# Six key chunks of a pair scored in one group of 64-row matmuls, and a new instruction order for attention and the experts

## The chip, the cores and the metric

The kernel runs on one core of a Trainium2 chip. The metric is the device time of one execution in microseconds (us). Engines are named as in the profile: PE (TensorE matmul), PEld (its weight load), DVE (VectorE), ACT (ScalarE), POOL (GpSimd), SP (SyncE, here a DMA queue).

## What is computed

Attention over four batches of eight heads (768 positions, head size 64), with a local band of |distance| < 16 and 24 block summaries per head; its result goes through a gate that is normalised eight times over rows and columns, and through eight experts that all see every token.

```python
k_sum = k.reshape(B, H, nb, 32, D).max(axis=3)
v_sum = v.reshape(B, H, nb, 32, D).mean(axis=3)
scores_l = scale * q @ k^T, kept where |i - j| < 16
scores_s = scale * q @ k_sum^T + log(32)
a = softmax(concat[scores_l, scores_s]);  x = a @ concat[v, v_sum]     # 3072 x 512
P = exp(x @ w_gate);  8 times: rows to 1, columns to N / E
out = sum over e of P[:, e] * (relu(x @ w1[e]) @ w2[e])                # 512 -> 1024 -> 512
```

## The kernel before

**Attention** works on 16 pairs of heads, four per batch. Pairs 0 to 3 (batch 0) go in halves of 384 positions (`pair_half`, L731), so that the first expert can start early; pairs 4 to 15 go whole (`pair_whole`, L761). The steps of a whole pair are: transposes of k and q (`tr`, `tr_out`; by a DMA transpose on SP from pair 12 on, `tr_dma`), `key_max`, `block_sums` and `block_out`, four small DMAs on SP (`near_values`), then for each half h: `scores` (three key chunks for each of the two heads), `score_exp` (ACT), `masks` (DVE); then `edges` (DVE), `summaries` and `summary_exp`, `values` (PE), `normalize` (DVE), and the transposition of x (`to_xT` and `x_out`, or `x_dma` on SP).

A score has a contraction of 64, so two heads share the array: head 0 uses rows 0 to 63 and head 1 rows 64 to 127 (`score_mm`, L388). All other matmuls, but the first transposes, use all 128 rows. `scores` writes head 0 into one bank of the two-bank PSUM buffer `s` and head 1 into the other (columns 0 to 479 of each):

```python
def scores(i, h):
    sg = at["sg", i, h] = banks2("sg")
    for s in range(HG):          # three chunks
        for j in range(2):       # two heads
            score_mm(i, sg[:, j, s * LIVE:(s + 1) * LIVE], j, HG * h + s, 0, LIVE)
```

PSUM has eight banks: `m` three, `a` three, `s` one buffer of two. Expert 0's products (`hidden0` into `m`, `project0` into `m`) are done as plain matmuls between the steps of attention, batch by batch, as its rows of x come in. Its relu and its copies out may go to ACT or DVE.

**The gate** needs all of x. Its eight normalisations (`bridge`, L1495) are a chain of small DVE, POOL and PE steps beside expert 0's last matmuls and expert 1's first ones. `bridge` starts with three 128x512 matmuls on zeros (L1498).

**Experts 1 to 7** use Winograd's seven products for both matrix products (`duo`, `pair`), in places with a second level (`second`, L1050; `twin`, L1378). Each product's PSUM bank is copied or combined by ACT and DVE between matmuls that go into it: `p1`, `seed`, `p2` and so on, in `plan_duo`; `q1`, `c1` (L1203), `q5`, `v5`, `q6`, `v6` (L1216) and so on in `plan_pair`. Results go out as accumulating DMAs on POOL (`da`, `db`, L1287 and L1290), and in the last block by SP and ACT queues (`store`, L1239).

**The order** is no written sequence. Each step is a unit with an engine, a cost in us, its dependencies, a priority and PSUM buffers; `Plan.order` (L60) puts units out one by one, always the one that can start first by those costs and, among those that can start within 0.02 us of it, the one of lowest priority value. A unit on PE that changes the shape of the array (64-row, 64-column or whole) costs `RESHAPE` = 0.1 more. Where PE would stand idle for over 0.22 us before the first relu, the planner puts in a 128x512 matmul on zeros (`keep_busy`, L597). The result is a fixed order of instructions on each engine; each engine takes its own in order and waits on semaphores. In attention the priorities are pair numbers; for the experts they are numbers in a table `PR`.

Of the kernel before, what the change touches and what calls it, by code (L numbers as in the profile page):

```python
# [36 lines left out]
class Plan:  # L37

    HOP = {"PE": 0.23}
    RESHAPE = 0.1  # L40

    def __init__(self, slots, idle=None):
        self.idle, self.shape = idle, None
        self.ring, self.free, self.waiting, self.now = {}, {}, [], []
        self.more(slots)
# [14 lines left out]
    def order(self):  # L60
# [3 lines left out]
        def hop(x, e):  # L64
            return 0.0 if x.on == e else self.HOP.get(x.on, 0.1)

# [20 lines left out]
        while waiting or left:  # L87
# [4 lines left out]
            for u in left:  # L92
                t0 = ready(u)
# [11 lines left out]
            for e, c in best.items():  # L105
                t_min = min(t for t, _, _ in c)
                t, u, cost = min((x for x in c if x[0] <= t_min + 0.02), key=lambda x: (
                    not (e == "PE" and self.shape and x[1].shape), x[1].prio))
                picks.append((t, t + cost, e, u, cost))
# [31 lines left out]
def kernel(  # L141
# [111 lines left out]
    if True:  # L253
# [175 lines left out]

        def score_exp(i, h):  # L430
# [262 lines left out]
        def pair_start(i, prio):  # L693
# [4 lines left out]
            for z in range(2 if i >= PB else 1):  # L698
# [9 lines left out]
                U["kT", i, z] = add({"ACT": 0.8} if z == 0 else {"ACT": 0.8, "DVE": 0.95},  # L708
# [4 lines left out]
            U["km", i] = add("DVE", 0.85, lambda: key_max(i), [U["kT", i, 0]] + war_q[2:], prio)  # L713
# [5 lines left out]
            U["Vs", i] = add("DVE", 0.24 if i < PB else 0.7, lambda: block_out(i), [U["vs", i]],  # L719
                             prio + 0.01, uses=[buf])  # L720

        def query_half(i, h, prio):
# [4 lines left out]
            U["kT", i, 1] = add({"ACT": 0.46, "DVE": 0.5}, 0, lambda: tr_qh_out(U["qT", i, h].on, i, h),  # L727
# [3 lines left out]
        def pair_half(i, h, prio):  # L731
            if h:
# [6 lines left out]
                               [U["kT", i, 0], U["kT", i, 1], hist("mk", n - 3), hold], prio, opens=[buf], shape="row")  # L739
            U["X", i, h] = add("ACT", 1.0, lambda: score_exp_h(i, h), [U["S", i, h]], prio, uses=[buf])  # L740
            U["mk", i, h] = add("DVE", 0.78, lambda: masks_h(i, h),
# [5 lines left out]
            U["sx", i, h] = add("ACT", 0.46, lambda: summary_exp(i, h), [U["ss", i, h]], prio, uses=[buf])  # L747
            buf = Buffer("a")
            U["A", i, h] = add("PE", 0.67, lambda: values_h(i, h),
                               [U["mk", i, h], U["sx", i, h], U["Vs", i]], prio, opens=[buf])  # L750
            U["no", i, h] = add("DVE", 0.68, lambda: normalize(i, h), [U["A", i, h], hist("xt", n - 2)],
                                prio, uses=[buf])
            buf = Buffer("a")
            U["xt", i, h] = add("PE", 0.172, lambda: to_xT(i, h), [U["no", i, h], U["gc"]], prio, opens=[buf])
            U["x", i, h] = add({"ACT": 0.46, "DVE": 0.5}, 0, lambda: x_out(U["x", i, h].on, i, h),
# [4 lines left out]

        def pair_whole(i, prio):  # L761
            U["near", i] = add("SP", 2.5, lambda: near_values(i), [U["v", i], U.get(("A", i - NE, 1))], prio,
                               lag=4.5)
            for h in range(2):
                buf = Buffer("s")
                U["S", i, h] = add("PE", 0.215, lambda h=h: scores(i, h),
                                   [U["kT", i, 0], U["kT", i, 1], U.get(("ed", i - 2))], prio, opens=[buf], shape="row")
                U["X", i, h] = add("ACT", 0.97, lambda h=h: score_exp(i, h), [U["S", i, h]], prio, uses=[buf])
                U["mk", i, h] = add("DVE", 0.56, lambda h=h: masks(i, h),
                                    [U["X", i, h], U.get(("A", i - 2, 1))], prio)  # L770
            U["ed", i] = add("DVE", 0.78, lambda: edges(i),
                             [U["X", i, 0], U["X", i, 1], U["mk", i, 1], U.get(("A", i - NE, 1))], prio)
            for h in range(2):
                buf = Buffer("a")
                U["ss", i, h] = add("PE", 0.17, lambda h=h: summaries(i, h, "a"),
                                    [U["km", i], U["kT", i, 1], U.get(("A", i - NE, 1))], prio, opens=[buf])
                U["sx", i, h] = add("ACT", 0.46, lambda h=h: summary_exp(i, h), [U["ss", i, h]], prio, uses=[buf])
            for h in range(2):
                buf = Buffer("a")
                U["A", i, h] = add("PE", 0.36, lambda h=h: values(i, h),  # L780
                                   [U["mk", i, h], U["ed", i], U["sx", i, h], U["Vs", i], U["near", i]],
                                   prio, opens=[buf])
                U["no", i, h] = add("DVE", 0.68, lambda h=h: normalize(i, h),
                                    [U["A", i, h], U.get(("xt", i - 2))], prio, uses=[buf])
# [3 lines left out]
            else:  # L788
                buf = Buffer("a")
                U["xt", i] = add("PE", 0.34, lambda: to_xT(i), [U["no", i, 0], U["no", i, 1]], prio, opens=[buf])  # L790
                U["x", i] = add({"ACT": 0.8, "DVE": 0.9}, 0, lambda: x_out(U["x", i].on, i), [U["xt", i]], prio,
# [4 lines left out]
        def expert0(t0, xs):  # L796
# [5 lines left out]
            for f in range(KF):  # L802
# [13 lines left out]
                U["rl", key, f] = add({"ACT": 0.5, "DVE": 0.56}, 0, ev, [m], -1.0, uses=[buf])  # L816
                evac.append(U["rl", key, f])
                zero.extend([m, evac[-1]])
            for c in range(HG):
# [9 lines left out]
                U["yo", key, c] = add({"ACT": 0.58, "DVE": 0.68}, 0, ev, [p1], -1.0, uses=[buf])  # L829
                zero.extend([p0, p1, U["yo", key, c]])  # L830

        def gate(b, xs, prio):
            buf = Buffer("a")
            U["lg", b] = add("PE", 0.61, lambda: logits(b), xs, prio, opens=[buf])
            U["lo", b] = add("ACT", 0.25, lambda: logits_out(b), [U["lg", b]], prio, uses=[buf])
# [72 lines left out]
        plan.idle = (0.22, lambda: keep_busy(1), U["rl", 0, 0])  # L908
        attention = {u for u in plan.waiting if u.fn is not None} - set(zero)
# [11 lines left out]
    if True:  # L921
# [444 lines left out]
        def twin(e, j, c, b0, b1):  # L1366
# [49 lines left out]
            def n4():  # L1416
# [4 lines left out]
        us = dict(m=0.1092, p=0.4316, q=0.4368, seed=0.55, c5=0.5, c2=0.49, r=0.49, c12=0.607, c22=0.607, s=0.6,  # L1421
                  n=0.2232, ns=0.6, nw=0.205, c1=0.34, v6=0.28, v5=0.35, y=0.395, half=0.275, join=0.335, w1=0.205, w2=0.6, wa=0.14, x=0.6,
                  xa=0.2, sc=0.63, part=0.36, da=1.0)
# [137 lines left out]
        for u in course:  # L1561
# [371 lines left out]
```

## Time and profile before

| what | value |
|---|---|
| median of three runs | 661.84 us (660.36 to 662.11) |
| the profiled execution | 661.13 us, of which the span from the first to the last instruction is 659.1 us |
| granted TensorE clock | 1.000 |
| PE busy | 650.6 us, 5575 matmuls |
| DVE busy | 546.6 us |
| ACT busy | 528.0 us |
| POOL busy | 260.2 us |
| DMA | 77.73 MB, 118 GB/s on average |

Attention with expert 0 between its steps takes the first 110 us; expert 0 alone with the gate goes on to 175 us; experts 2 to 6 repeat a pattern of 71.4 us; the last expert ends at 655 us, and DMAs to 659.1 us. A matmul's bar in the trace is longer than the time until the next one starts (matmuls are pipelined), so waits shorter than about 0.16 us do not show as idle time; they show in the distance between the starts of matmuls.

### The profile page before, as it was taken

How to read it: one execution, taken by the hardware profiler on the slowest of the kernel's cores; microseconds unless marked ns; L12 is line 12 of the kernel's file. 1: busy time of each engine (PE TensorE's matmuls, PEld its weight loads, DVE VectorE, ACT ScalarE, POOL GpSimd, SP SyncE). 2: the span in 40 equal slices, each digit the busy share in tenths (PEclk: the TensorE clock that was granted, in tenths of full speed). 3: DMA queues.
4: the chain of work that ended last, by engine and by line, in shares of the span. 5: the costliest groups of instructions: out<-in, count | busy, mean ns of one | idle time of the engine just before them, and what ended most of it. 6: DMA issues, size and time to landing. Idle time of an engine off the chain costs nothing.

```text
span 659.1 us, 15106 instructions
## 1 busy us (share of the span) xinstructions
PE 650.6 (99%) x5575; PEld 446.3 (68%) x5575; DVE 546.6 (83%) x1356; ACT 528.0 (80%) x1183; POOL 260.2 (39%) x320
## 2 busy tenths in 40 slices
PE   8999999999999999999999999999999999999997
PEld 4766656555677766676776776767767677676676
DVE  8889998678799979896898779877889689876876
ACT  6776766565996578889898898898989989888872
POOL 8599504223101022444345244433344335633421
PEclk9999999999999999999999999999999999999999
DMA  9999957700727357986989698977998699978758
GB/s 162 185 148 149 148 85 77 93 2 1 143 68 141 123 99 106 111 109 92 173 103 118 93 141 124 117 101 106 158 108 112 93 175 128 137 110 191 113 85 190
DMA packets 147368, 77.73 MB, mean 118 GB/s; under 512 B 112736, under 2 KB 125280, under 8 KB 147296
## 3 DMA queue, kind: packets, MB, share of 16 engines
q0 software_dynamic: 124864, 62.64, 80.9%
q1 hardware_dynamic: 21472, 13.68, 8.4%
q8 instruction: 43, 0.70, 0.5%
q10 hardware_dynamic: 960, 0.48, 0.3%
q14 instruction: 29, 0.24, 0.1%
HBM read 55.59 MB, written 45.09 MB: 153 GB/s over the span
## 4 chain that ended last, share of the span: by engine, by line
PE 86%; DVE 7%; DMA 3%; issue 1%; POOL 1%; ACT 0%; DVEq 0%; POOLq 0%
PE pab L992 16%; PE pg L992 16%; PE py L998 16%; PE px L998 13%; PE px L1378 7%; PE yps L236 5%; PE hps L226 5%; PE pab L1050 4%; DVE xs L552 1%; DMA kT<-kst 1%; DMA w<-in_moe_w_dram 1%; DMA kst<-in_k_dram 1%; PE sg L388 1%; PE tkq L354 1%; DVE em L440 1%
## 5 line engine op out<-in xcount | busy, mean ns | idle before, releaser
L998 PEld LDWEIGHTS <-hf 128*128 128x128 f16 x1840 | 178.4, 98 | 53.2
L1290 POOL DMA_DIRECT2D out_dram<-out_acc x68 | 62.0, 917 | 173.8 <-ACT out_acc L1266 141.2
L936 DVE TENSOR_TENSOR hf<-hf 128x1024 f16<-128x1024 f16 x142 | 94.6, 692 | 4.1 <-ACT hf L217 1.4
L998 PE MATMUL py<-w,hf 128*128 128x256 f16 x656 | 92.6, 273 | 0.0
L1287 POOL DMA_DIRECT2D out_dram<-out_acc x68 | 64.9, 955 | 56.3 <-ACT out_acc L1266 27.2
L942 DVE CUSTOM_DVE_ANT_0 hf<-pg,c 128x512 f16<-128x512 f32 x84 | 57.5, 684 | 28.5 <-PE pg L992 15.6
L1266 ACT ACTIVATE out_acc<-py,P_sb 128x256 f32<-128x256 f32 x136 | 65.3, 490 | 6.9 <-PE py L998 6.8
L992 PEld LDWEIGHTS <-ws 128*128 128x128 f16 x504 | 47.5, 98 | 31.6 <-issue 0.3
L202 POOL DMA_DIRECT2D w<-in_moe_w_dram x56 | 44.6, 844 | 49.1 <-PE pg L992 46.8
L992 PEld LDWEIGHTS <-w 128*128 128x128 f16 x520 | 48.1, 98 | 21.7 <-issue 0.6
L1116 ACT COPY c<-pab 128x512 f32<-128x512 f32 x84 | 50.1, 596 | 15.9 <-PE pab L992 14.5
L942 DVE CUSTOM_DVE_ANT_0 hf<-pab,c 128x512 f16<-128x512 f32 x84 | 57.5, 685 | 6.2 <-ACT c L1123 3.4
L998 PE MATMUL px<-ws,hf 128*128 128x256 f16 x400 | 59.8, 273 | 0.0
L217 ACT ACTIVATE hf<-pg 128x512 f16<-128x512 f32 x84 | 50.6, 602 | 11.3 <-PE pg L992 10.5
L998 PE MATMUL px<-w,hf 128*128 128x256 f16 x400 | 59.3, 273 | 0.0
L992 PE MATMUL pab<-xT,w 128*128 128x512 f16 x184 | 54.4, 379 | 0.0
L1108 ACT COPY pg<-pab 128x512 f32<-128x512 f32 x84 | 49.7, 592 | 3.4 <-PE pab L1050 3.0
L1123 ACT COPY c<-pg 128x512 f32<-128x512 f32 x84 | 49.7, 591 | 3.3 <-PE pg L992 1.5
L217 ACT ACTIVATE hf<-pab 128x512 f16<-128x512 f32 x84 | 49.8, 610 | 3.0 <-PE py L998 2.0
L992 PE MATMUL pg<-xTs,w 128*128 128x512 f16 x168 | 50.0, 379 | 0.1
L992 PE MATMUL pg<-xTs,ws 128*128 128x512 f16 x168 | 50.0, 379 | 0.0
L992 PE MATMUL pab<-xT,ws 128*128 128x512 f16 x168 | 50.0, 379 | 0.0
(190 smaller groups left out, 1511.2 us busy)
## 6 DMA issues: line engine op xcount, KB each, us to landing
out_dram<-out_acc POOLq DMA_DIRECT2D x136, 256.0 KB, 5.1
w<-in_moe_w_dram POOLq DMA_DIRECT2D x8, 1024.0 KB, 11.2
w<-in_moe_w_dram POOLq DMA_DIRECT2D x56, 128.0 KB, 5.0
out_dram<-out_acc SPq DMA_DIRECT2D x28, 256.0 KB, 2.3
vx<-in_v_dram POOLq DMA_DIRECT2D x16, 192.0 KB, 5.8
qst<-in_q_dram POOLq DMA_DIRECT2D x31, 96.0 KB, 5.3
kst<-in_k_dram POOLq DMA_DIRECT2D x24, 96.0 KB, 5.4
out_acc<-out_dram SPq DMA_DIRECT2D x8, 256.0 KB, 4.0
```

What stands on the lines that cost most here:

```text
L217: nc.scalar.activation(out=out, in_=in_, func=AF.Relu, bias=0.0, scale=1.0)
L936: nc.vector.tensor_tensor(out=out, in0=in0, in1=in1, op=ALU.subtract)
L942: nc.vector._custom_dve(TENSOR_ADD_SAT, out=out, in0=in0, in1=in1, s0=FLT_MAX, s1=0.0)
L992: nc.tensor.matmul(bank[:], lhsT=w[:, dk, :], rhs=x[:, dk, :], start=start and dk == 0, stop=dk == KH - 1, skip_group_check=True)
L998: nc.tensor.matmul(bank, lhsT=a(f)[:, 128 * c:128 * (c + 1)], rhs=w[:, f, :], start=start and f == 0, stop=f == FH - 1, skip_group_check=True)
L1108: nc.scalar.copy(out=B["g" + K][:], in_=B["a" + K][:])
L1116: nc.scalar.copy(out=B["c5" + K][:], in_=B["b" + K][:])
L1123: nc.scalar.copy(out=B["c2" + K][:], in_=B["g" + K][:])
L1266: nc.scalar.activation(out=out_acc[:, (c, HT + c)[t == tb], k * DH:(k + 1) * DH], in_=at(src), func=AF.Copy, scale=scale[:, t, e:e + 1])
L1287: nc.gpsimd.dma_start(out=rows(ta), in_=out_acc[:, c, :], accum_op=ALU.add)
L1290: nc.gpsimd.dma_start(out=rows(tb), in_=out_acc[:, HT + c, :], accum_op=ALU.add)
L1378: nc.tensor.matmul(half(b, k)[:, g, :], lhsT=still2(e, j, g, w, c)[:, i, :], rhs=moving2a(e, g, v)[:, i, :], start=start and g == 0 and i ...
```

## The change

The scores of a whole pair are one unit of twelve matmuls instead of two of six. Chunks 0 to 2 still go to the buffer `s`; chunks 3 to 5 go to one `m` bank (head 0) and one `a` bank (head 1). The exponential of the first half stays one instruction over both heads (128x960); that of the second half becomes two of 128x480. `scores_h` of pairs 0 to 3 is as before.

```diff
+def scores_all(i):
+    sg = at["sg", i, 0] = banks2("sg")
+    one = at["sg", i, 1] = [bank(t, "sg") for t in ("m", "a")]
+    for h in range(2):
+        for s in range(HG):
+            for j in range(2):
+                dst = one[j][:, s * LIVE:(s + 1) * LIVE] if h else sg[:, j, s * LIVE:(s + 1) * LIVE]
+                score_mm(i, dst, j, HG * h + s, 0, LIVE)
+
+def score_exp_j(i, j):
+    nc.scalar.activation(out=at["er", i][:, j, HG:G, :].rearrange("p g l -> p (g l)"),
+                         in_=at["sg", i, 1][j][:, 0:HG * LIVE], func=AF.Exp, bias=0.0, scale=SCALE)
...
 def pair_whole(i, prio):
+    bufs = [Buffer("s"), Buffer("m"), Buffer("a")]
+    U["S", i, 0] = U["S", i, 1] = add("PE", 0.43, lambda: scores_all(i), [...], prio, opens=bufs, shape="row")
+    U["X", i, 0] = add("ACT", 0.97, lambda: score_exp(i, 0), [U["S", i, 0]], prio, uses=bufs[:1])
+    ex = [add("ACT", 0.48, lambda j=j: score_exp_j(i, j), [...], prio, uses=bufs[1 + j:2 + j]) for j in range(2)]
+    U["X", i, 1] = add("LAND", 0, None, ex, lag=-0.1)
     for h in range(2):
-        buf = Buffer("s")
-        U["S", i, h] = add("PE", 0.215, lambda h=h: scores(i, h), [...], prio, opens=[buf], shape="row")
-        U["X", i, h] = add("ACT", 0.97, lambda h=h: score_exp(i, h), [U["S", i, h]], prio, uses=[buf])
         U["mk", i, h] = add("DVE", 0.56, lambda h=h: masks(i, h), [...])
```

The rest changes what the planner works with, and so the order alone: other costs, other waits between engines, a dependency of each step on the same step of the pair before (S, X, A, no, xt), a table `RANK` of some 400 numbers added to the priorities of attention's units, a new `PR` table (same names, other numbers), w1 loads reckoned as 4.3 us, and, in the Winograd sums, T3 or S3 no longer depending on the sum before it (`PREV`).

```diff
-    HOP = {"PE": 0.23}
+    HOP = {"PE": 0.23, "ACT": 0.15, "DVE": 0.14}
...
-U["rl", key, f] = add({"ACT": 0.5, "DVE": 0.56}, 0, ev, [m], -1.0, uses=[buf])
+U["rl", key, f] = add({"ACT": 0.39, "DVE": 0.475}, 0, ev, [m], -1.0, uses=[buf])
...
+RANK = {"k": -3.72, "q0": 5.3, "q0.0": 12.32, "v": 16.47,
...
+for key, u in U.items():
+    if isinstance(key, tuple) and u not in seen and u in plan.waiting:
+        kind = key[0] + "".join(str(x) for x in key[2:])
+        u.prio += RANK.get(kind, 0.0) + RANK.get(f"{kind}.{key[1]}", 0.0)
...
-us = dict(m=0.1092, p=0.4316, q=0.4368, seed=0.55, c5=0.5, c2=0.49, r=0.49, ..., c1=0.34, v6=0.28, v5=0.35,
+us = dict(m=0.1092, p=0.4316, q=0.4368, seed=0.53, c5=0.48, c2=0.48, r=0.485, ..., c1=0.27, v6=0.29, v5=0.335,
...
 def bridge():
-    for n in (0, 1, 0):
+    for n in (0, 1):
         nc.tensor.matmul(t[n][:], lhsT=zeros[:], rhs=zeros[:, None, :].to_broadcast([128, 4, 128]),
+    plan.HOP, plan.window = {"PE": 0.23}, 0.02
...
 PR = {
-    "m1": 2568.5, "m5": 1010.4, "m2": -2957.6,
+    "m1": -1176448.7, "m5": -881981.4, "m2": -883425.6,
...
+plan.SAME = {"DVE": 0.07}
+PREV = (None, 0, 0, 1)
```

In the two orders as built, compared engine by engine: PE has the same matmuls but for `bridge` (two on zeros instead of three) and `keep_busy` (27 on zeros instead of 24). Ten relus of expert 0 (of 17), three 128x384 copies and one 128x512 copy move from DVE to ACT. POOL's first 157 instructions (waits not counted), all of attention's loads among them, stand as before. On SP the k transposes of pairs 13 and 14, and q transposes with them, stand ahead of `near_values` of pairs 10 and 11.

More of the change, by code (lines that the diff above doesn't have):

```diff
@@ L37 @@
 class Plan:
[L39 removed]
+    HOP = {"PE": 0.23, "ACT": 0.15, "DVE": 0.14}
     RESHAPE = 0.1
+    SAME = {}
     def __init__(self, slots, idle=None):
[L43 removed]
+        self.idle, self.shape, self.window = idle, None, 0.02
         self.ring, self.free, self.waiting, self.now = {}, {}, [], []
@@ L707, in pair_start @@
                                     prio, opens=[buf], shape="col" if i < PB else None)
-                U["kT", i, z] = add({"ACT": 0.8} if z == 0 else {"ACT": 0.8, "DVE": 0.95},
+                U["kT", i, z] = add({"ACT": 0.7} if z == 0 else {"ACT": 0.7, "DVE": 0.475},
                                     0, lambda z=z: tr_out(U["kT", i, z].on, i, z), [U["tr", i, z]], prio,
@@ L712, in pair_start @@
                 query_half(i, 0, prio)
-            U["km", i] = add("DVE", 0.85, lambda: key_max(i), [U["kT", i, 0]] + war_q[2:], prio)
+            U["km", i] = add("DVE", 1.14, lambda: key_max(i), [U["kT", i, 0]] + war_q[2:], prio)
             if i == 0:
@@ L726, in query_half @@
                                 opens=[buf], shape="col")
-            U["kT", i, 1] = add({"ACT": 0.46, "DVE": 0.5}, 0, lambda: tr_qh_out(U["qT", i, h].on, i, h),
+            U["kT", i, 1] = add({"ACT": 0.4, "DVE": 0.475}, 0, lambda: tr_qh_out(U["qT", i, h].on, i, h),
                                 [U["tr", i, 1]], prio, uses=[buf])
@@ L738, in pair_half @@
             U["S", i, h] = add("PE", 0.225, lambda: scores_h(i, h),
-                               [U["kT", i, 0], U["kT", i, 1], hist("mk", n - 3), hold], prio, opens=[buf], shape="row")
-            U["X", i, h] = add("ACT", 1.0, lambda: score_exp_h(i, h), [U["S", i, h]], prio, uses=[buf])
-            U["mk", i, h] = add("DVE", 0.78, lambda: masks_h(i, h),
+                               [U["kT", i, 0], U["kT", i, 1], hist("mk", n - 3), hist("S", n - 1), hold], prio, opens=[buf], shape="row")
+            U["X", i, h] = add("ACT", 0.9, lambda: score_exp_h(i, h), [U["S", i, h], hist("X", n - 1)], prio, uses=[buf])
+            U["mk", i, h] = add("DVE", 0.71, lambda: masks_h(i, h),
                                 [U["X", i, h], U["band"], hist("A", n - NEH), clear], prio)
@@ L759, in hist, with before @@
             return U.get((what, n % PB, n // PB)) if n >= 0 else None
+        def before(what, i, h):
+            return U[what, i, 0] if h else U.get((what, i - 1, 1))
         def pair_whole(i, prio):
@@ L780, in pair_whole @@
                 U["A", i, h] = add("PE", 0.36, lambda h=h: values(i, h),
-                                   [U["mk", i, h], U["ed", i], U["sx", i, h], U["Vs", i], U["near", i]],
+                                   [U["mk", i, h], U["ed", i], U["sx", i, h], U["Vs", i], U["near", i], before("A", i, h)],
                                    prio, opens=[buf])
-                U["no", i, h] = add("DVE", 0.68, lambda h=h: normalize(i, h),
-                                    [U["A", i, h], U.get(("xt", i - 2))], prio, uses=[buf])
+                U["no", i, h] = add("DVE", 0.7, lambda h=h: normalize(i, h),
+                                    [U["A", i, h], U.get(("xt", i - 2)), before("no", i, h)], prio, uses=[buf])
             if 10 <= i < 15:
@@ L790, in pair_whole @@
                 U["xt", i] = add("PE", 0.34, lambda: to_xT(i), [U["no", i, 0], U["no", i, 1]], prio, opens=[buf])
-                U["x", i] = add({"ACT": 0.8, "DVE": 0.9}, 0, lambda: x_out(U["x", i].on, i), [U["xt", i]], prio,
+                U["x", i] = add({"ACT": 0.7, "DVE": 0.475}, 0, lambda: x_out(U["x", i].on, i), [U["xt", i]], prio,
                                 uses=[buf])
@@ L828, in ev @@
                     copy(U["yo", key, c].on, out_acc[:, t0 // 128 + c, :], at.pop(("yp", key, c))[:])
-                U["yo", key, c] = add({"ACT": 0.58, "DVE": 0.68}, 0, ev, [p1], -1.0, uses=[buf])
+                U["yo", key, c] = add({"ACT": 0.485, "DVE": 0.61}, 0, ev, [p1], -1.0, uses=[buf])
                 zero.extend([p0, p1, U["yo", key, c]])
@@ L1674, in h_sub_sums @@
                                       [src[0]["s2"], src[0]["s3"]], [])):
-                s.append(put("DVE", us["ns"], lambda n=n: h_sub(e, j, n), s[-1:] + more, prio + 0.01 * n))
+                s.append(put("DVE", us["ns"], lambda n=n: h_sub(e, j, n), ([s[PREV[n]]] if n else []) + more, prio + 0.01 * n))
         def w2_sub_sums(e, prio, old=()):
```

62 lines of the change are left out of this document (37 added, 25 removed), and 200 rows, old and new, of tables (PR, RANK).

## Prediction

> **What bounds the kernel now.** First the page's head, its busy shares and the chain that ended last.
>
> ```profile
> span 659.1 us, 15106 instructions
> ...
> PE 650.6 (99%) x5575; PEld 446.3 (68%) x5575; DVE 546.6 (83%) x1356; ACT 528.0 (80%) x1183; POOL 260.2 (39%) x320
> ...
> PE 86%; DVE 7%; DMA 3%; issue 1%; POOL 1%; ACT 0%; DVEq 0%; POOLq 0%
> ```
>
> PE is busy for 99% of the span and makes up 86% of the chain: PE's own time is the kernel's time. Work taken from DVE or ACT is worth nothing unless PE waits for it. Then busy times by stretch: start, attention with expert 0, gate, experts to 597 us, last expert, tail.
>
> ```profile
> 0.00:21.00 21.00, 18.00 (x243) 10.49 (x244) 16.80 (x100) 12.93 (x20) 17.36 (x28) 1.00 1.42 169
> 21.00:126.00 105.00, 104.00 (x1165) 65.68 (x1164) 92.07 (x279) 74.03 (x127) 60.33 (x76) 1.00 1.56 130
> 126.00:175.00 49.00, 49.00 (x282) 27.52 (x280) 35.60 (x83) 31.77 (x62) 13.37 (x19) 1.00 0.24 39
> 175.00:597.00 422.00, 421.83 (x3407) 299.77 (x3406) 357.16 (x807) 367.71 (x879) 150.33 (x178) 1.00 0.81 117
> 597.00:655.00 58.00, 57.73 (x486) 42.83 (x484) 43.96 (x88) 41.52 (x98) 18.78 (x22) 1.00 0.78 143
> 655.00:659.10 4.10, 0.00 (x0) 0.00 (x0) 1.00 (x3) 0.00 (x0) 0.00 (x0) 1.00 0.57 196
> ```
>
> The columns are the stretch, its length, then busy time (and count) of PE, PEld, DVE, ACT, POOL. PE has no idle time worth a name from 21 to 655 us. What can be won is of three kinds: PE time that does no work though PE looks busy, the start, and 4.1 us behind the last matmul. For the first I read PE's timeline round two score groups.
>
> ```profile
> 53.97 1.02 PE L236 MATMUL yps<-w,h 128*128 128x512 f16 x4
> 54.92 0.38 PE L388 MATMUL sg<-qT,kT 64*128 64x160 bf16 x6
> 55.24 1.90 PE L236 MATMUL yps<-w,h 128*128 128x512 f16 x8
> 56.98 0.35 PE L463 MATMUL av<-vx,em 128*128 128x65 bf16 x6
> ```
>
> The eight `yps` matmuls start 56.98 - 55.24 = 1.74 us before what follows, 0.217 each. The four ahead of the scores take 54.92 - 53.97 = 0.95, so 0.95 - 4 x 0.217 = 0.08 to 0.10 us (0.096 in the unrounded starts) pass when PE goes from whole array to 64 rows. The six scores take 0.32: two heads start 0.003 apart, so three pairs at 0.069 make 0.21, and 0.11 is left, again 0.096 for the way back and 0.01 for the first pair. A group thus pays 0.19 us for its two changes, whatever its length.
>
> The start, and a wait in the experts:
>
> ```profile
> 15.11 0.34 PE L475 MATMUL ss<-qT,ksT 128*128 128x384 bf16 x1
> 15.81 0.34 PE L559 MATMUL tx<-ident,xs 128*128 128x128 f16 x3 [0.36 <-DVE xs L552]
> ...
> 20.79 0.65 PE L226 MATMUL hps<-xT,w 128*128 128x384 f16 x3
> ```
>
> ```profile
> 305.95 1.04 PE L998 MATMUL py<-w,hf 128*128 128x256 f16 x8
> ...
> 306.52 0.43 DVE L939 TENSOR_TENSOR pab<-pab,m 128x256 f32<-128x256 f32 x1
> ...
> 307.00 0.27 PE L1050 MATMUL pab<-xT,wa 128*128 128x256 f16 x1
> ```
>
> Expert 0's first matmuls start at 20.79; until then PE mostly follows loads and DVE. In the experts eight matmuls at 0.109 end issue at 306.82, and PE goes on at 307.00, 0.05 after the DVE join ended: 0.18 us that a busy bar hides. Summed over all starts between 174 and 655 us, such waits come to 2.3 us, of them 0.9 behind 597 us.
>
> **The change part by part.** (1) *Grouped scores.* Twelve pairs lose one group each: 24 changes of shape. In the two orders PE changes shape 74 times before and 50 after. 24 x 0.096 = -2.30 us. It lies on the path, since PE is without idle time there. Below it could be 0 only if the second six paid as much inside the group; inner distances in the groups of eight of pairs 0 to 3 (0.066 to 0.069 a pair throughout) speak against that.
>
> (2) *One matmul on zeros less* in `bridge`: 512 columns, -0.22 us.
>
> (3) *Split exponential.* From 478 ns (64x384) and 970 ns (128x960) a line gives 560 ns for 128x480: 24 x 0.56 - 12 x 0.97 = +1.8 us of ACT. Ten relus (0.49), three copies (0.48) and one wide copy (0.59) come from DVE: +6.9. ACT in 21 to 126 us goes from 74.0 to 82.7 of 105, DVE from 92.1 to some 84 (13 x 0.55 and 0.6 less). Both stay under PE, so 0. With that cover gone the split would add its 1.8. The Trainium skill, page "ScalarE: Activation LUTs", section "What ACT_TABLE_LOAD costs", gives an ACTIVATE with a pointer bias about 280 ns and 0.833 ns an element: an estimate of 0.68 us for 480, so +3.4 us in place of 1.8; uncovered, the sum below would be +0.7 by the page and -0.9 by the rows. The trace bears the rows out (960 wide: 0.97, where the page's figures give 1.08).
>
> (4) *The start.* From the transposes of pair 1 (released by a load that landed at 8.6 us, POOL's order being unchanged) to 20.79 PE waits 1.5 us in all beyond its work and its fills. The two largest, 0.53 before 15.81 and 0.29 behind it, are for `normalize` (L552) of pair 1, which stands behind four `key_max` steps on DVE; the new order puts it ahead of them, and `normalize` of pair 0 ahead of three memsets. Also 0.33 us of block sums move ahead of the wait at 8.6, and one more fill (0.22) comes behind it: -0.11. Ends: all 1.5 waits gone (-1.6); nothing gained and the three extra fills paid in full (+0.65). I take the two named waits: -0.82 - 0.11 = -0.9.
>
> (5) *Attention's waits otherwise.* A score group now holds four banks until three exponentials (0.97 + 2 x 0.56) are done, the `m` bank among expert 0's three. On SP two or more transposes (1.2 to 1.3 us of queue each) are put ahead of `near_values` of pairs 10 and 11, whose consumer `values` stands some 10 us of PE work on; four issues take 2.5 us and a landing 3.0 (median; 6.6 the longest). The shortest such distance is 7.6 us now, 9.4 before. Ends: -0.4 (the short waits now between 21 and 126 us go) and +1.5 (2.5 + 6.6 - 7.6). I take the median landing, which leaves 2 us over, and 0.1 for small waits.
>
> (6) *The new expert order.* PE's work is the same. For each matmul that waits for ACT or DVE I take the PE work that the order puts between it and the matmul that released the producer, less the shortest need in the trace (for `c1`, L1203: 0.20 us from matmul to copy and 0.455 from the copy's start to PE). What is left is a reserve for queueing. Against the waits of the trace (before), and in the new order:
>
> | reserve, us | places before | of them waited | us waited | places now |
> |---|---|---|---|---|
> | under 0.1 | 20 | 0 | 0 | 51 |
> | 0.1 to 0.2 | 72 | 9 | 1.3 | 90 |
> | 0.2 to 0.5 | 296 | 8 | 0.5 | 233 |
> | over 0.5 | 268 | 2 | 0.2 | 222 |
>
> A reserve near nothing costs nothing by itself: those 20 met their time. By row the new order has 1.65 + 0.4 + 0.2 = 2.2 us of waits for 2.0 in the table before; one of its places, a DVE join in the last expert, is 0.24 short of its need. Together +0.4. Ends: -2.3 (all waits go) and +2.9 (the 31 more places under 0.1 wait 0.08 each besides, what the nineteen above waited on average, 2.0 / 19, rounded down).
>
> (7) *The tail.* DVE's last steps start 0.39 us apart, the first 0.20 after its product. Before, eight steps follow from the product that ends five products (5 x 0.436 = 2.18) ahead of PE's end: -2.18 + 0.20 + 8 x 0.39 = 1.14 us behind it. Now four follow from the one that ends 0.44 ahead: -0.44 + 0.20 + 4 x 0.39 = 1.32. The last stores are 256 KB on SP and 128 KB on ACT's queue (median landing 2.6 and 2.4) instead of 128 KB on SP (2.2). Ends 0 and +0.5; I take +0.2.
>
> Sum: -2.30 - 0.22 - 0.9 + 0.1 + 0.4 + 0.2 = **-2.7 us**. The profiled execution took 661.13 us, its span 659.1: 658.4 and 656.4. The median of the runs shown is 661.84, 0.7 above it, so **659.1 us** for the median.
>
> **The rivals.** *Both orders pay* (657.3): the start gives 1.6 and the experts lose 0.7 of their waits, so -2.7 - 0.7 - 1.1 = -4.5. For it: DVE is relieved in attention, and fewer places lie between 0.2 and 0.5; against: those under 0.2 grow from 92 to 141. *The experts take it back* (661.6): term 6 at +2.9, so -2.7 + 2.5 = -0.2. For it: 51 places without reserve, ACT busy 87% between 175 and 597 us (367.7 of 422); against: the 20 before never waited. *Score banks hold PE up*: slower. Place: each whole pair's group needs its four banks free, and PE, in order, stops at its first matmul until the exponentials of another pair (2.1 us) have run. Price 12 x the wait; at 0.22 us a pair it eats the gain, from 0.39 us on the kernel is over 2 us slower; at 0.4 us -2.7 + 4.8 = +2.1: 663.9. For it: ACT gets 8.7 us more in this stretch and the `s` buffer is single; against: ACT has 22 us free there, and the new order leaves PE work between. The Trainium skill, "TensorEngine Tiling (Array Packing)", section "Gotcha 1: PSUM Pressure", has row tiles of one group write to different banks and names the pressure as the price; no run here shows that yet. *The grouping saves nothing* (pairs in single banks follow each other more slowly by what the changes cost): -0.4: 661.4.
>
> **How the numbers follow.** Forecast 0.54, both pay 0.16, taken back 0.20, banks 0.06, no saving 0.04. A measurement of this kernel tells 0.3%, 2.0 us, from no change (the three runs lie within 1.75 us): faster means under 659.85. The forecast with its own spread of about 0.9 us is under that four times in five: 0.43; with "both pay" 0.16 and a quarter of "taken back" 0.05: 0.64. Slower is the banks' case and a little of "taken back": 0.07; the rest, 0.29, is no change. The range reaches from both orders paying, less 0.5, to the taken-back cases: 656.8 to 661.8; the forecast's own is 658.1 to 660.3.
>
> **What would show it.** PE: 12-matmul groups of `sg` taking some 0.09 in and 0.52 to the next matmul, not 2 x 0.41; expert 0's first matmul near 19.9 us; two `bridge` matmuls; waits in the experts that sum to some 2.5 us; last matmul to end of span 4.3 us. The forecast is wrong if PE waits before `sg` groups or at `values` for `Ve`, if the first `hps` comes at 20.8 or later, or if the pattern of 71.4 us an expert grows by over 0.2 us.

## The result and the profile after

The changed kernel took 660.19 us (median of 22 runs, 658.22 to 661.52), the kernel before 661.73 us beside it (22 runs): a ratio of 0.9974, with a 95% interval of 0.9965 to 0.9982. It is faster by 0.26% (0.18 to 0.35%): a gain clear of zero, and just under the 0.3% that the prediction set as the line to "faster". The profiled execution took 659.39 us (661.13 before). One execution among those told of below, of the kernel no_late_stores, took 2397.92 us and is left out of its row. The head of the page of the changed kernel, the busy times and the chain that ended last:

```profile
span 657.5 us, 15072 instructions
...
PE 647.5 (98%) x5577; PEld 447.0 (68%) x5577; DVE 536.0 (82%) x1342; ACT 533.4 (81%) x1209; POOL 255.7 (39%) x320
...
PE 94%; DVE 2%; DMA 1%; ACT 1%; issue 0%; SPq 0%; DVEq 0%
```

The span is 1.60 us shorter, but PE's share of it fell from 99% to 98%: some of the end is now without PE. Where the time went is seen from the starts of the matmuls. "Waits" are the distances between starts, less what a matmul of that shape takes in an undisturbed row; in the attention (from expert 0's first matmul to the last `av`) those at a change of shape are kept apart. How much falls to each of these two rows depends on what is taken as undisturbed (another count gives -2.17 and -2.01); their sum, -4.1 to -4.2, hardly does.

| stretch, us | before | after | difference |
|---|---|---|---|
| start, to expert 0's first matmul | 20.79 | 20.65 | -0.14 |
| attention: excess at changes of shape (59, 35 of them) | 6.79 | 4.21 | -2.58 |
| attention: PE's other waits | 4.67 | 3.12 | -1.55 |
| bridge, by counting | 0.65 | 0.43 | -0.22 |
| experts: PE's waits | 3.02 | 3.16 | +0.14 |
| last matmul's start to the end of the span | 4.55 | 7.38 | +2.83 |
| last matmul's start | 654.58 | 650.15 | -4.43 |

PE was done 4.4 us earlier, and 2.8 us of that were given back behind its last matmul. First the score groups, in PE's timeline:

```profile
52.91 0.34 PE L483 MATMUL av<-Ve,Ee 128*128 128x130 bf16 x3
53.18 0.59 PE L389 MATMUL sg<-qT,kT 64*128 64x160 bf16 x12
53.70 1.04 PE L237 MATMUL yps<-w,h 128*128 128x512 f16 x4
```

Twelve score matmuls stand in one group. They take 53.70 - 53.18 = 0.52 us with the change back, and 0.10 lies ahead of them (53.18 - 52.91, less three of 0.056): six pairs at 0.069 and two changes. The second six pay nothing inside the group. So twelve groups less save about 12 x 0.2 = 2.4 us. The busy times of the attention's stretch, in the order PE, PEld, DVE, ACT, POOL:

```profile
21.00:126.00 105.00, 104.56 (x1185) 68.08 (x1184) 88.83 (x274) 80.18 (x153) 59.56 (x79) 1.00 1.56 130
```

DVE lost 3.2 us there (92.1 before) and ACT gained 6.2 (74.0 before). Whom PE waited for in this stretch, by the view of waits (total, times, longest), before and after:

```profile
PE tx L559 <- DVE xs L552: 0.3, 1, 0.3
PE vs L398 <- DVE xs L552: 0.3, 1, 0.3
PE ss L475 <- DVE xs L552: 0.2, 1, 0.2
```

```profile
PE sg L389 <- DMA qT<-qst: 0.3, 1, 0.3
```

Before, PE stood for `normalize` (`xs`) of DVE three times; with what the long bars hide, the four longest waits there came to 1.51 us (at 50.73, 64.47, 93.29 and 104.69). None of them is left. The one wait shown after the change, 0.39 us start to start at 87.23, stands before a score group: its q came by a DMA transpose on SP. The start, in PE's timeline of the changed kernel:

```profile
15.99 0.34 PE L489 MATMUL ss<-qT,ksT 128*128 128x384 bf16 x1 [0.25 <-DVE ksT L384]
...
18.64 0.38 PE L611 MATMUL idle<-zeros 128*128 128x512 bf16 x1
19.16 0.34 PE L573 MATMUL tx<-ident,xs 128*128 128x128 f16 x3
...
20.65 0.65 PE L227 MATMUL hps<-xT,w 128*128 128x384 f16 x3
```

The two waits for `normalize` that the prediction named are gone, and two others stand in their place: 0.41 us at 15.99 for the last step of `key_max`, which `normalize` was put ahead of on DVE, and 0.31 at 19.16 (the fill at 18.64 covers 0.22 of the time) for the `normalize` of another pair. Last, the end: the DMA queues from the start of the last matmul to the end of the span (MB and share of 16 engines; then KB each and us to landing), before and after:

```profile
q1 hardware_dynamic: 720, 0.79, 50.1%
...
out_dram<-out_acc SPq DMA_DIRECT2D x1, 256.0 KB, 2.3
```

```profile
q1 hardware_dynamic: 982, 1.39, 51.3%
q0 software_dynamic: 56, 0.08, 6.1%
...
q8 instruction: 1, 0.02, 0.8%
...
out_dram<-out_acc SPq DMA_DIRECT2D x1, 256.0 KB, 4.4
```

After the last matmul SP's queue has 1.39 MB to move instead of 0.79, POOL's queue still runs, and a store takes 4.4 us to land instead of 2.3. POOL's timeline shows why its queue runs so late, before and after:

```profile
641.17 0.86 POOL L1287 DMA_DIRECT2D out_dram<-out_acc  x1 [5.30 <-ACT out_acc L1266]
641.81 1.11 POOL L1290 DMA_DIRECT2D out_dram<-out_acc  x1
645.30 0.86 POOL L1290 DMA_DIRECT2D out_dram<-out_acc  x1 [2.38 <-DVE out_acc L1271]
648.66 0.86 POOL L1287 DMA_DIRECT2D out_dram<-out_acc  x1 [2.50 <-ACT out_acc L1266]
```

```profile
642.86 0.85 POOL L1367 DMA_DIRECT2D out_dram<-out_acc  x1 [11.02 <-ACT out_acc L1346]
643.40 2.07 POOL L1370 DMA_DIRECT2D out_dram<-out_acc  x2
644.48 1.87 POOL L1367 DMA_DIRECT2D out_dram<-out_acc  x1
```

These are `da` and `db`, the stores of 256 KB that add to the output in DRAM. Before, the last four start 13.4, 12.8, 9.3 and 5.9 us ahead of PE's last matmul; now POOL stands idle for 11 us and then starts all four 7.3 to 5.7 us ahead of it, since the new order puts the last expert's second block's last five products behind those of a pair of its third block. What this does to the 16 DMA engines shows in their busy tenths, 40 slices of 0.45 us each: before from 642 to 660 us, after from 640 to 658.

```profile
DMA  0896999962895979999963998899888999300000
```

```profile
DMA  0089880009279999999999999999999821000000
```

Before, about the same bytes are spread over 15 us, with gaps. After, the engines stand idle from 642.7 to 644 us and are then busy for 90% or more from 645.4 to 654, past PE's last matmul at 650.15.

### The profile page after: what moved, and what is told of

It reads as the page before. It is cut to its first block, busy times and chain, and to the rows that moved or that the text cites. A ratio compares the mean times of both kernels' runs of the same rounds, so it can differ in the third digit from the quotient of the medians.

```text
span 657.5 us, 15072 instructions
## 1 busy us (share of the span) xinstructions
PE 647.5 (98%) x5577; PEld 447.0 (68%) x5577; DVE 536.0 (82%) x1342; ACT 533.4 (81%) x1209; POOL 255.7 (39%) x320
## 4 chain that ended last, share of the span: by engine, by line
PE 94%; DVE 2%; DMA 1%; ACT 1%; issue 0%; SPq 0%; DVEq 0%
PE pab L1072 17%; PE pg L1072 16%; PE py L1078 16%; PE px L1078 13%; PE px L1458 8%; PE hps L227 6%; PE yps L237 6%; PE pab L1130 4%; DMA qT<-qst 1%; PE sg L389 1%; PE idle L611 1%; PE tkq L355 1%; PE ss L489 1%; PE av L477 1%; PE av L483 1%; PE pab L1078 1%
## 5 line engine op out<-in xcount | busy, mean ns | idle before, releaser
L1078 PEld LDWEIGHTS <-hf 128*128 128x128 f16 x1840 | 177.4, 98 | 50.2
L1078 PE MATMUL py<-w,hf 128*128 128x256 f16 x656 | 94.8, 273 | 0.0
L1016 DVE TENSOR_TENSOR hf<-hf 128x1024 f16<-128x1024 f16 x142 | 92.8, 687 | 0.0
L1346 ACT ACTIVATE out_acc<-py,P_sb 128x256 f32<-128x256 f32 x136 | 63.0, 488 | 8.4 <-PE py L1078 7.3
L1072 PEld LDWEIGHTS <-w 128*128 128x128 f16 x520 | 50.2, 99 | 25.2 <-issue 0.6
L1019 DVE TENSOR_TENSOR px<-px,out_acc 128x256 f32<-128x256 f32 x64 | 27.3, 427 | 33.6 <-PE px L1458 33.6
L1458 PEld LDWEIGHTS <-hf 128*128 128x128 f16 x512 | 38.6, 98 | 16.9 <-issue 0.2
```

Source lines behind the costliest of these rows:

```text
L1016: nc.vector.tensor_tensor(out=out, in0=in0, in1=in1, op=ALU.subtract)
L1072: nc.tensor.matmul(bank[:], lhsT=w[:, dk, :], rhs=x[:, dk, :], start=start and dk == 0, stop=dk == KH - 1, skip_group_check=True)
L1078: nc.tensor.matmul(bank, lhsT=a(f)[:, 128 * c:128 * (c + 1)], rhs=w[:, f, :], start=start and f == 0, stop=f == FH - 1, skip_group_check=True)
L1346: nc.scalar.activation(out=out_acc[:, (c, HT + c)[t == tb], k * DH:(k + 1) * DH], in_=at(src), func=AF.Copy, scale=scale[:, t, e:e + 1])
L1458: nc.tensor.matmul(half(b, k)[:, g, :], lhsT=still2(e, j, g, w, c)[:, i, :], rhs=moving2a(e, g, v)[:, i, :], start=start and g == 0 and i ...
```

## The experiments

The planner's choices shift with everything ahead of them, so to change one half alone the experts' 3743 steps were emitted in an order read from a list, taken from the other kernel:

```diff
-        for u in plan.order():
+        for i, *now in ORDER:
+            u = plan.made[base0 + i]
+            plan.now = now
             if u.fn is not None:
                 u.fn()
```

All results in one table; "end" is from the start of the last matmul to the end of the span in the profiled execution.

| kernel | median, us (runs) | ratio to before, 95% interval | last matmul | end |
|---|---|---|---|---|
| changed | 660.19 (22) | 0.9974 [0.9965, 0.9982] | 650.15 | 7.38 |
| attn_only | 658.09 (6) | 0.9940 [0.9923, 0.9958] | 651.97 | 4.41 |
| exp_only | 663.80 (12) | 1.0027 [1.0016, 1.0038] | 654.76 | 7.42 |
| two_groups | 662.08 (12) | 1.0000 [0.9989, 1.0012] | 652.62 | 8.31 |
| group_only | 663.92 (5) | 1.0038 [1.0026, 1.0050] | 657.76 | 4.37 |
| no_rank | 663.63 (11) | 1.0023 [1.0013, 1.0033] | 654.31 | 8.01 |
| relu_back | 663.08 (9) | 1.0023 [1.0014, 1.0032] | 653.25 | 7.34 |
| old_tail | 656.88 (6) | 0.9938 [0.9924, 0.9952] | 649.99 | 4.38 |
| no_late_stores | 657.80 (4) | 0.9942 [0.9930, 0.9955] | 651.28 | 5.51 |
| early_stores | 664.57 (6) | 1.0043 [1.0029, 1.0056] | 658.36 | 4.88 |
| early_stores2 | 658.00 (6) | 0.9946 [0.9929, 0.9963] | 651.65 | 5.81 |
| fewer_fills | 659.38 (12) | 0.9968 [0.9952, 0.9983] | 650.23 | 6.23 |
| early_fewer | 658.75 (7) | 0.9957 [0.9940, 0.9974] | 652.09 | 4.88 |

**Each half alone.** Expected of the first:

> The changed kernel's start, attention with expert 0 and gate, followed by the Strassen experts in exactly the order of the kernel before. Theory A (the attention half earns 4.3 to 4.6 us until PE's last matmul, and the stores behind it are late because of the new expert order): last matmul near 650.0 us, from there to the end of the span 4.5 us instead of 7.4, span near 654.6, median near 657.3 us, 0.66% under the kernel before. Rival B (the 7.4 us behind the last matmul belong to the one execution profiled or to anything but the expert order): the tail stays near 7.4 and the median near 660.2.

and of the second:

> The kernel before up to the gate, followed by the Strassen experts in exactly the order of the changed kernel. Theory A: PE's waits in the experts change by under 0.3 us, the tail grows from 4.55 to about 7.4 us, span near 662.1, median near 664.6, 0.4% over the kernel before. Rival B: tail near 4.5, median near 661.8. Rival C (the new expert order earns what its reserves suggest at best): last matmul 2 us earlier than before.

The ends fell out as theory A has them, 4.41 and 7.42 us: the late end goes with the expert order, and the rival by which it belonged to one execution falls. The new expert order alone makes the kernel slower by 0.27%, less than the 0.4% expected. The median of attn_only was 0.8 us above what was expected, because PE waited 2.1 us at 287.28 (start to start). PE's waits, and DVE's:

```profile
PE pg L1074 <- DVE hf L1024: 1.9, 1, 1.9
```

```profile
DVE ws L1021 <- DMA w<-in_moe_w_dram: 2.4, 1, 2.4
```

A load of expert weights came too late. The kernel before waited at the same place for 0.28 us (289.94); with PE some 4.5 us earlier the load kept up with only part of that. The new expert order has no such wait: with the faster attention ahead of it, PE needs 1.8 us less from the last `av` to the last matmul (542.7 us against 544.5), and only its end is dearer.

**The price of a change of shape.** In `scores_all`:

```diff
             for h in range(2):
+                if h:
+                    nc.tensor.matmul(one[0][:, 0:16], lhsT=zeros[:], rhs=zeros[:, 0:16], start=True, stop=True)
                 for s in range(HG):
```

> The changed kernel, in the same order, with one 128-row matmul on zeros (16 columns) between the two halves of each of the twelve whole-pair score groups, so that PE changes its array shape 24 times more, as before the change. Theory A (each change costs 0.10 us on PE's path): 24 x 0.1 and 12 x 0.03 for the extra matmuls, +2.8 us until the last matmul, median near 663. Rival B (waits for ACT and DVE would have been there instead, or the changes are hidden): under +0.5 us, median near 660.4.

From expert 0's first matmul to the last `av` it took 89.08 us in place of 86.80, 2.28 us more. That is a little less than the price of the changes: each of the twelve groups is 0.22 us longer, start to start, 2.66 us in all with the small matmuls, and the 0.39 us wait for q at 87.23 is missing in this run. So a change costs about 0.1 us. Rival B falls. The last matmul came 2.47 us later, the median is 1.9 us above the changed kernel's.

**Grouping alone, and ranks.** The first is the kernel before with `scores_all`, `score_exp_j` and the new `pair_whole` units but the old estimates; the second is the changed kernel with

```diff
-                u.prio += RANK.get(kind, 0.0) + RANK.get(f"{kind}.{key[1]}", 0.0)
+                pass
```

> The kernel before with the grouped scores and the split exponential alone: the old estimates of durations, no ranks by hand, and the experts in exactly the order of the kernel before. Theory A (the shape changes alone earn 0.107 us each, the rest of the attention half's gain came from the order and from the steps moved to ACT): 24 x 0.107 = -2.6 us in the attention's shape changes, PE's other waits in the attention at 4.7 us or more as before, median near 659.5. Rival B (the four banks of a group hold PE up unless the order is made for them): PE's waits there grow by over 2 us, median 661.5 or more. Rival C (the grouping itself takes the waits for normalize away): waits near 3.1, median near 658.

> The changed kernel with the ranks by hand taken out (its new durations and dependencies stay, its experts run in exactly its order). Theory A (the new durations, which move relus and copies from DVE to ACT, make the order): PE's waits in start and attention grow by under 1 us, median 661 or less. Rival B (the ranks place the work so that the exponentials and normalize are never waited for): the waits in the attention, 3.1 us with the ranks, come to 5 us or more, median 662.5 or more.

Grouping alone made the kernel slower than before by 0.38%. The excess at changes of shape fell by 2.47 us, as theory A has it, but PE's other waits in the attention rose from 4.67 to 9.61 us: rival B. The longest, in the view of waits:

```profile
PE tkq L356 <- ACT er L442: 1.1, 1, 1.1
PE av L478 <- ACT er L442: 1.0, 1, 1.0
```

L442 is the split exponential: the next group of transposes stands at its `m` bank, and `values` at the `a` bank whose scores it has not yet taken. This is the rival "score banks hold PE up" of the prediction, in a kernel whose order is not made for it, though PE stops at the next users of the banks and not at the group's first matmul. These two waits, 2.5 us start to start, are about half of the increase; the other half is for steps of DVE (copies of q, `Ve`, relus), so it isn't the banks alone. The Trainium skill, page "TensorEngine Tiling (Array Packing)", section "Gotcha 1: PSUM Pressure", says that the row tiles of a group write to different banks and that this presses on PSUM; the trace agrees, with idle times of 1.14 and 1.05 us at 62.23 and 65.78, both for a bank. Taking only the ranks out cost 4.2 us until the last matmul: 1.2 in the start and 2.8 in the attention, of them 1.56 at changes of shape and 1.26 in other waits. The waits reached 4.4, not the 5 of rival B, but the median did what that rival said: the durations alone do not make the order. Without the ranks the planner also gave relus back to DVE (12 there in the first 126 us, 6 in the changed kernel, 14 before), so this run does not tell the places of the steps from their engines.

**Relus moved to ACT.** The same order, with expert 0's relus and copies out on their old engines (the moved copies of q and x stay on ACT):

```diff
-                    relu(U["rl", key, f].on, at["h", key][:, f, 0:HS], at.pop(("hp", key, f))[:, 0:HS])
+                    relu(OLD.get((key, f), U["rl", key, f].on), at["h", key][:, f, 0:HS], at.pop(("hp", key, f))[:, 0:HS])
```

> The changed kernel in the same order, with the relus and copies of expert 0 that changed their engine put back (13 relus and 3 copies from ACT to DVE, 3 relus and 2 copies from DVE to ACT). Theory A (PE's four long waits for normalize went because DVE has 5 us less to do in the attention): PE's waits there grow from 3.1 to 4.2 us or more, median 661.3 or more. Rival B (the order took them away): they grow by under 0.3 us, median near 660.4.

PE's other waits in the attention rose from 3.1 to 7.1 us, the stretch from 86.80 to 90.64. The view of waits names DVE first:

```profile
PE hps L227 <- DVE h L220: 1.0, 2, 0.6
```

Rival B falls. Start to start, PE's waits for DVE there are 1.4 us for relus put back, 0.9 for `normalize`, 0.5 for copies of q and 0.5 for masks and edges. The size is an upper end, since this order was made for steps on ACT.

**The end.** For old_tail the list is the changed kernel's up to the last expert's second block, and from there the kernel before's. For no_late_stores `da` and `db` of that block leave out pairs 1 and 3:

```diff
-                nc.gpsimd.dma_start(out=rows(ta), in_=out_acc[:, c, :], accum_op=ALU.add)
+                if (e, j) != (E - 1, NJ - 2) or c % 2 == 0:
+                    nc.gpsimd.dma_start(out=rows(ta), in_=out_acc[:, c, :], accum_op=ALU.add)
```

For the two with early stores the list has these products in another order, with the steps that take them (block and pair of the last expert):

```diff
-q6 2.3 | q1 3.3 | q5 3.3 | q1 3.1 | q5 3.1 | q2 2.3 | q6 3.3 | q4 q2 q3 q7 3.3 | q4 3.1 | q4 q7 q3 2.3 | q4 q3 2.1
+q6 2.3 | q4 q3 2.1 | q1 3.3 | q5 3.3 | q1 3.1 | q5 3.1 | q2 2.3 | q6 3.3 | q4 q7 q3 2.3 | q4 q2 q3 q7 3.3 | q4 3.1
```

> The changed kernel up to the second block of the last expert (613 us), then the rest of the last expert's work in the relative order of the kernel before. Theory A (the late end belongs to the order of the last expert's products and stores, by which the last four accumulating stores start together 7.3 us before PE's last matmul): last matmul near 650.2, 4.5 us from there to the end, span 654.7, median near 657.2, 0.7% under the kernel before. Rival B (it belongs to something earlier): the end stays 6.2 us or more behind the last matmul, median 659 or more.

> The changed kernel without the last four accumulating stores (2 x 2 of 256 KB, second block of the last expert; half of that block's share of the output is left out). Theory A (they share the DMA engines with the last stores and hold these up): from the last matmul to the end 4.5 to 5.5 us in place of 6.2 to 8.3, median 658 or less. Rival B (the last stores hold themselves up): 6.2 us or more, median near 660.

> The changed kernel with one edit to the order: the last five products of the last expert's second block (pairs 1 and 3), the steps on ACT and DVE that take them, and the four accumulating stores behind these are put ahead of the products of the third block's pair 3, so that the four stores start some 13 to 9 us before PE's last matmul in place of 7.3 to 5.7. Nothing is left out. Theory A (the four late accumulating stores hold up the end): 4.4 to 5.5 us from the last matmul to the end (7.3 without the edit), PE's last matmul as before the edit to within 0.5 us, median 657 to 658.5. Rival B (the order of the last stores proper decides): 6.2 us or more, median near 660.

> As the run with the same edit before it, but with pair 3's fourth step on DVE and its store behind the step on ACT that fills the same rows, so that no store stands ahead of what it is to write: the four accumulating stores start some 13 to 8 us before PE's last matmul. Nothing is left out. Theory A (the four late accumulating stores hold up the end): 4.4 to 5.5 us from the last matmul to the end (7.3 without the edit), PE's last matmul within 0.7 us of the changed kernel's, median 657 to 658.7. Rival B (the order of the last stores proper decides): 6.2 us or more, median near 660.

With the old order for the last 37 us the end came 4.38 us behind the last matmul, and the kernel took 656.88 us: 0.62% (0.48 to 0.76) under the kernel before, the lowest median here. Leaving the four stores out gave an end of 5.51 us, starting them early 5.81: both under the 6.2 of rival B, and a little over the 5.5 of theory A. In early_stores2 the last matmul came 1.5 us later than in the changed kernel, not within 0.7: 0.3 of it lies in the start and 0.7 in the attention, whose order is the same, and 0.5 is a wait of PE at 642.60 in the edited stretch. early_stores, the first of these two, says nothing by its median: in its order `e4` and the store of pair 3 stood ahead of `e2`, which fills the same rows (so those rows are not what they should be), and ACT waited for the store, then PE 5.7 us for ACT (its last matmul came 8.2 us after the changed kernel's):

```profile
ACT out_acc L1348 <- DMA out_dram<-out_acc: 5.1, 1, 5.1
```

**The instruction packet.** In the changed kernel one packet of 16 KB (q8, above) falls among the last stores, takes 0.95 us on one DMA engine, and from 655.3 us on the last store packets, up to 655.95, follow each other one at a time. For fewer_fills the last three fills of the start are left out, for early_fewer the same beside the early stores:

```diff
-        plan.idle = (0.22, lambda: keep_busy(1), U["rl", 0, 0])
+        fills = iter([1] * 16 + [0] * 99)
+        plan.idle = (0.22, lambda: keep_busy(next(fills)), U["rl", 0, 0])
```

> The changed kernel, in the same order, without the last three matmuls on zeros ahead of expert 0's first matmul (at 19.34 us). Theory A (they stand in a wait of PE for pair 3 and cost nothing): expert 0's first matmul stays at 20.6 us. Rival B (they hold PE up): it comes at 20.0. And with six instructions less on PE: Theory C (the 44th 16 KB instruction packet, at 653.0 us, delays one DMA engine's last stores by 1 us, and is there only because PE's program is just long enough): 43 such packets, the last store packet about 1 us earlier, median 659.2 at A. Rival D: still 44, or the end unchanged.

> The run before this one (four accumulating stores early, nothing left out) without the last three matmuls on zeros ahead of expert 0. Theory A (what is left of the late end beside the accumulating stores, 5.8 us against 4.4, is one 16 KB instruction packet among the last stores, 0.14 us behind PE's last matmul there, and six PE instructions less move it behind the end): end 4.4 to 5.1 us behind the last matmul, median near 657. Rival B (the order of the last stores proper makes it): 5.5 us or more, median near 658.

In fewer_fills there are still 44 packets, but the last moved behind the end, and the end came 1.15 us earlier; in early_fewer it is gone from the end, 4.88 us against 5.81. Against it stands relu_back: its last packet falls behind the end too, and its end is 7.34 us, as late as the changed kernel's with the packet. And where the packet falls doesn't follow PE's count of instructions alone, as theory C had it: old_tail has as many PE instructions in its trace as the changed kernel, 11211, and no packet at its end. Expert 0 began at 20.35 (fewer_fills) and 21.01 (early_fewer) instead of 20.65 us without the fills, and the last matmul came no earlier; other executions of the same start lie between 20.36 and 21.12, so neither A nor B is shown. The end by run, in us against the start of the last matmul:

| kernel | last four adding stores start | their last packet | instruction packet near the end | end |
|---|---|---|---|---|
| before, attn_only, group_only, old_tail | -13.4 to -5.9 | -1.5 to -0.9 | none | 4.4 to 4.6 |
| early_fewer; early_stores | -12.7 to -8.6; -20.1 to -11.3 | -2.6; -7.6 | none | 4.88; 4.88 |
| early_stores2 | -12.7 to -8.5 | -2.9 | +0.1 | 5.81 |
| no_late_stores | left out | | +0.1 | 5.51 |
| fewer_fills, relu_back | -7.3 to -5.7 | +1.2, +2.4 | none | 6.23, 7.34 |
| changed, exp_only, no_rank, two_groups | -7.3 to -5.7 | +1.6 to +3.4 | +0.8 to +2.8 | 7.38 to 8.31 |

With the four stores late the end is 6.2 to 8.3 us, with them early or out 4.9 to 5.8. Of what is left, 0.6 to 0.9 us go with the packet in these traces (5.51 and 5.81 against 4.88), and 0.4 are left for the new order of the last stores (4.88 against 4.4 to 4.6). The packet's part is not shown: each end is that of one execution, relu_back speaks against it, and the medians of early_stores2 and early_fewer (658.00 and 658.75) don't differ beyond their intervals.

## Why the prediction came out as it did

It forecast 659.1 us, 2.7 less than before, in a range of 656.8 to 661.8; measured were 660.19 and a gain of 1.5 us between the medians, 1.7 by the ratio. The range held and the sign was right. That the number came this near is in part luck: measured less forecast, the terms missed by +2.63 us (tail), +0.76 (start), -1.65 (attention's other waits), -0.28 (grouped scores) and -0.26 (experts), +1.2 together.

- **Grouped scores, -2.30:** right. 24 changes less gave -2.58 in the changed kernel (-2.17 by the other count), -2.47 alone, and putting them back cost 2.28 net and 2.66 by the groups themselves.
- **Bridge, -0.22:** right by counting; not measured by itself.
- **Split exponential and moved steps, 0:** wrong. The exponential of 128x480 took 0.56 us as worked out. But the text said that work taken from DVE is worth nothing unless PE waits for it, and PE did wait for it: relu_back shows that without DVE's relief the new order loses 4.0 us to waits, most of them for DVE. That the relief alone would have kept `normalize` in time is not shown: in relu_back 0.9 us of the waits are for it, in no_rank 1.4. The cover was asked after for ACT and not for DVE.
- **Start, -0.9:** wrong. "I take the two named waits" took their end for gain; on the same DVE queue a step for PE stood behind each (`key_max`, the next `normalize`). Eight profiles with the new start have expert 0 at 20.73 us on average (20.36 to 21.12), three with the old at 20.74: no gain.
- **Attention's other waits, +0.1:** wrong in sign, -1.55. The low end counted the short waits as -0.4; start to start, the four longest alone were 1.51, and the experts had been summed that way. The place named for a loss was right: in early_fewer PE waited for `near_values` of a pair (below). In the profile of the changed kernel it did not, but it waited 0.39 us before a score group for a transpose of q on the same queue, one of the signs that the prediction had named.

```profile
PE av L485 <- DMA Ve<-vx: 0.7, 1, 0.7
```

- **New expert order, +0.4:** near: +0.14 of waits in the changed kernel. That it would spare a 2 us wait for a load behind the faster attention was not seen.
- **Tail, +0.2:** this is the step that failed most: +2.83. DVE's last step started 1.06 us behind the last matmul (1.32 forecast), so the chain that was priced was right. The term priced the last stores alone and took their landing from the old trace, though the four stores on POOL's queue had moved into the same 7 us.

Of the rivals, the score banks' mechanism is real: it came about in group_only, and not in the changed kernel, whose order is made for the groups; "grouping saves nothing" is excluded by two_groups. "Both orders pay" falls with the start (-0.14) and the experts (+0.14). "Experts take it back" names the right side of the loss and the wrong engine: PE lost nothing there, the DMA engines did.

## What to carry to other kernels

A change of array shape is worth taking out where PE has no idle time, but grouping holds more banks at once: alone it lost more than it gained here, and the order has to be made for it. A step that leaves a busy engine isn't free of effect because another engine is the bound: look for waits, start to start, that name the engine it leaves. When an order is changed, list for the last 15 us of the kernel which transfers start when, on all queues; time won on the bound engine is lost there if the stores arrive together.

## What the runs showed of the hardware

The stores that add in DRAM, on POOL's queue, held the DMA engines longer than the plain ones on SP's. In the changed kernel's last stretch (the view of queues from 640 to 657 us):

```profile
q0 software_dynamic: 576, 1.05, 39.7%
q1 hardware_dynamic: 1440, 1.84, 30.2%
```

q0 has the four adding stores: 39.7% of 17 us, 6.7 us of all 16 engines for 1.05 MB; q1 has plain ones, 5.1 us for 1.84 MB. A byte costs 2.3 times as much, and of packets of 2048 bytes the median one took 178 ns on q0 and 84 ns on q1. All stores on POOL's queue add and all on SP's are plain, so no run here tells the adding from the queue. The Trainium skill, page "DMA: Bandwidth & Descriptors", section "Rules for kernel authors", says that an accumulating DMA reads its destination and writes it later; the longer packets would fit that, but no run here shows the reading by itself. From 642.9 us on these queues had about 11 us of work for all engines (6.7 of q0, 1.44 of q1's 1.84 MB or 4.0, 0.4 of ACT's queue), and the last packets landed 655.95 - 642.9 = 13 us later; the engines were 90% busy or more from 645.4 to 654 us. So at the end it is the DMA engines that set the time, not PE.
